# Attention, norm and MLP in one kernel: 1 KB input pieces for batch 0, and the loads of the second batch and of both weights in another order

## The chip, the cores and the metric

The kernel runs on one core of a Trainium2 chip. The metric is the device time of one execution in microseconds (us). A run counts as fast unless it lies more than 1.5% above the fastest run of the same kernel. In the profiles PE is TensorE (PEld its weight loads), DVE is VectorE, ACT is ScalarE, POOL is GpSimd and SP is SyncE; PSUM is the memory that the products are written to, and "busy" is the time in which an engine ran instructions. Verdicts are at 2%: a change that gains less is called "same".

## The reference, cut to what matters

Eight batches of eight heads of causal attention (576 positions, 64 wide) with a bias from running sums of `s`, then, on the joined heads, a norm scaled by `g_ln`, an up product with relu, a down product, and a residual.

```python
scores = scale * np.matmul(q, k.transpose(0, 1, 3, 2))
cum = np.cumsum(np.maximum(s, 0.0), axis=-1)
bias = -(cum[:, :, :, None] - cum[:, :, None, :])
scores = np.where(causal, -1e9, scores + np.minimum(bias, 0.0))
x = softmax(scores) @ v                              # (8, 8, 576, 64), then joined to (8, 576, 512)
xn = (x - mu) / np.sqrt(var + 1e-06) * g_ln
out = x + np.maximum(xn @ w_ch1, 0.0) @ w_ch2        # w_ch1 512 x 2048, w_ch2 2048 x 512
```

## The kernel before

The 64 heads run one after the other; "head 11" below is head 3 of batch 1. From head 11 on, MLP products of the batch before are laid between a head's own products. q and k are transposed by TensorE and copied out of PSUM by DVE or ACT. The bias rides in the product as four extra rows: the running sums, split into three bf16 terms, and ones, so 68 rows instead of 64.

```python
QUADS = (1, 2)        # batches whose q and k come in 1 KB pieces (4 positions per partition)

def t_pe(b, h, engs=("dve", "dve")):       # q, then k, of one head into qkT
    if b in QUADS:
        return t_quads(b, h, engs)         # two copies that put the order right (68x512),
                                           # and a third for the last 64 positions (68x2x64)
    for j, eng in ((h, engs[0]), (H + h, engs[1])):
        ...                                # five transposes, one straight copy (68x640)
```

Inputs are issued by SP, in one queue, but for three of the first ones, which ACT issues; casts to bf16, causal masks and the issues of the weights (which are cast in flight) are POOL's. What stands where in the program is set by hooks: `at(g, pos, f)` runs `f` in head g.

```python
for c, g in enumerate((6, 6, 7, 7)):                    # w1 in four parts
    at(g, "a", lambda c=c: load_w1(c))
for h, g in enumerate((0, 0, 1, 1, 7, 7, 8, 8)):        # q, k, v of batch 1, head h
    at(g, "e", lambda h=h: b1_in(h))                    # (h == 2 also loads g, 256 KB)
for i, g in enumerate((10, 10, 11, 11)):                # w2 in four parts
    at(g, "b", lambda i=i: load_w2(i))
at(12, "c", lambda: split(2 * H, BH, nc.vector))        # the sums of batches 2 to 7
for g in (12, 13, 14):                                  # batch 2
    at(g, "a", lambda g=g: b2_in(g))
```

The softmax here doesn't subtract the row's maximum and nothing guards it: scores larger than these inputs give would overflow.

Of the kernel before, what the change touches and what calls it, by code (L numbers as in the profile page):

```python
# [16 lines left out]
def kernel(  # L17
# [36 lines left out]
    QUADS = (1, 2)  # L54
# [43 lines left out]

    scr = xbufs[0]
# [6 lines left out]
    nc.sync.dma_start(out=s_sb, in_=s.rearrange("b h s -> (b h) s"))  # L106

# [53 lines left out]
    def t_quads(b, h, engs):  # L161
        pts = [ps_m.tile([P, 2 * 512], BF16, name="pt", tag="pm") for _ in range(2)]
        tails = pts[1][0:DK, NF * P : NF * P + 2 * P].rearrange("r (j n) -> r j n", j=2)
        for i in range(2):
# [11 lines left out]
            "dve", qkT[b][0:DK, :, NF * P : S].rearrange("r (j h) n -> r j h n", j=2)[:, :, h, :],  # L176
            tails[:, :, 0:TL],
        )

    def t_pe(b, h, engs=("dve", "dve")):  # L180
        if b in QUADS:
            return t_quads(b, h, engs)
        for j, eng in ((h, engs[0]), (H + h, engs[1])):
            pt = ps_m.tile([P, 2 * 512], BF16, name="pt", tag="pm")
            for p in range(NT):
                nc.tensor.transpose(pt[0:DK, p * P : (p + 1) * P], aug[:, p, j, 0:DK], ident)  # L186
            copy(eng, qkT[b][0:DK, j, :], pt[0:DK, 0:SP_])
# [10 lines left out]
    def score_mms(g):  # L198
# [6 lines left out]
        def mm(o, kb, lo, hi):  # L205
            lhsT = qkT[b][0:DK, H + h, kb * P : (kb + 1) * P]
            w = 0
            if g < NPM and lo == kb * P:
                w = min(P, hi - lo)
                nc.tensor.matmul(  # L210
                    o[:, 0:w], lhsT=lhsT, rhs=qkT[b][0:DK, h, lo : lo + w], start=True, stop=False
                )
                nc.tensor.matmul(
                    o[:, 0:w], lhsT=ident, rhs=negm[:, 0:w], start=False, stop=True
                )
            if lo + w < hi:
                nc.tensor.matmul(  # L217
                    o[:, w:], lhsT=lhsT, rhs=qkT[b][0:DK, h, lo + w : hi], start=True, stop=True
                )
# [6 lines left out]
        mm(pot[:, 448:512], 4, 512, 576)  # L226
# [65 lines left out]
    def store(c, a, yo):  # L292
        if c >= B:
            b0 = 4 * (c - B) + 2 * a
            late.append((out[b0, NF * P : S, :], yo[0:TL]))
            late.append((out[b0 + 1, NF * P : S, :], yo[TL:P]))
        else:
            late.append((out[c, a * P : (a + 1) * P, :], yo))

    def stores(eng, keep=0):  # L300
        while len(late) > keep:
            o, i = late.pop(0)
            eng.dma_start(out=o, in_=i)
# [186 lines left out]
    def spin(n):  # L490
        for _ in range(n):
            nc.tensor.matmul(idle[:, 0:P], lhsT=ident, rhs=ident, start=True, stop=True)

    spin(44)
# [7 lines left out]
    pc = ps_m.tile([P, 512], F32, name="pc", tag="pm")  # L502
    for p in range(NT):
        nc.tensor.transpose(pc[:, p * BH : (p + 1) * BH], cum[:, p * P : (p + 1) * P], ident_f)
# [3 lines left out]
    pc_v = pc[:, 0 : NT * BH].rearrange("p (t c) -> p t c", c=BH)  # L508
# [13 lines left out]
    split(0, H, nc.vector, pc_v[:, :, 0:H], aug[:, :, H:HD, D1:DK])  # L522
# [5 lines left out]
    spin(8)  # L528
    t_pe(0, 0, ("act", "dve"))
    nc.scalar.copy(out=c8, in_=pc_v)  # L530

    def cum_quads():

        pq = ps_m.tile([P, 512], F32, name="pq", tag="pm")[:, 0 : NF * 3 * H]
        pq = pq.rearrange("p (t c) -> p t c", t=NF)
        cum_q = cum[0 : 3 * H, 0 : NF * P].rearrange("c (p t) -> c t p", t=NF)
        for p in range(NF):
            nc.tensor.transpose(pq[:, p, :], cum_q[:, p, :], ident_f[0 : 3 * H, 0 : 3 * H])
        qs = slice(QUADS[0] * H, (QUADS[-1] + 1) * H)
        nc.vector.tensor_copy(out=c8[:, 0:NF, qs], in_=pq[:, :, qs])  # L540
# [26 lines left out]
    def t_next(g):  # L567
        t_pe((g + 2) // H, (g + 2) % H, ("dve", "act" if g >= H else "dve"))
# [191 lines left out]
```

## Time and profile before

| | before |
|---|---|
| time, median of 3 runs (range) | 379.52 us (378.34 to 379.99) |
| the profiled run: time, span | 380.23 us, 378.5 us |
| PE busy over the span | 94% |
| start of heads 6, 11, 14, 16 | 23.25, 42.99, 59.58, 80.43 us |

The times were taken outside the profile and the span inside it, so the span is 1.7 us shorter. The starts are the first score product of each head in the trace's order of time. The profiled run is at the slow end of the runs of its kernel. The lines of the profile itself stand in the prediction (those of the trace: start, length, instruction, wait in brackets).

Two stretches; the columns are stretch, length, busy PE, PEld, DVE, ACT, POOL, clock, DMA share and GB/s.

```profile
20.00:30.00 10.00, 8.73 (x157) 7.54 (x158) 7.98 (x22) 5.87 (x12) 3.62 (x9) 1.00 0.60 159
52.00:56.00 4.00, 2.55 (x15) 1.20 (x14) 3.90 (x6) 2.23 (x4) 4.00 (x7) 1.00 0.60 81
```

In these two stretches the DMA engines are 60% busy. The second hole has its reason in POOL's order of time (start, length, instruction, wait in brackets):

```profile
51.69 0.45 POOL L127 CAST v_bf<-ring 128x320 bf16<-128x320 f32 x1 [2.24 <-DMA ring<-in_v_dram]
52.08 1.57 POOL L151 DMA_DIRECT2D w_bf<-in_moe_w_ch_dram  x2
```

### The profile page before, as it was taken

Reading aid. Unit: us, or ns where it says so; the run is one execution under the profiler, and the core shown is the slowest. Engines: PE = TensorE matmul, PEld = TensorE weight load, DVE = VectorE, ACT = ScalarE, POOL = GpSimd, SP = SyncE. Lnnn points to the kernel's source line nnn. Section 1 sums busy time; section 2 is a strip of 40 time slices with the busy share of each in tenths; the row PEclk is TensorE's granted clock in tenths of the full one; section 3 lists DMA queues with packets and bytes.
Section 4 is the critical chain, followed back from the end, with each engine's and each line's share of the span. In section 5 each row is a group of like instructions: output and inputs, shape, how many; then the busy total and the mean of one; then the engine's idle time right before and its main releaser. Section 6 shows DMA issues by size and latency. Waiting matters only on the chain.

```text
span 378.5 us, 7931 instructions
## 1 busy us (share of the span) xinstructions
PE 354.7 (94%) x3017; PEld 204.5 (54%) x3017; DVE 201.9 (53%) x466; ACT 163.9 (43%) x295; POOL 167.6 (44%) x328
## 2 busy tenths in 40 slices
PE   6987878888999999999999999999999999899994
PEld 5966645455555455545555755555555555344471
DVE  6788575765454544594447435733555353933131
ACT  3755755154563457335632546444623554031020
POOL 3537964493634545575455544463444111500000
PEclk9998999999999999999999999999999999999998
DMA  9958989997999789999999999599804001420202
GB/s 164 207 150 190 221 143 187 245 248 176 176 227 227 137 198 211 229 198 205 174 210 239 174 246 224 119 195 207 156 29 113 29 2 55 113 55 0 86 28 55
DMA packets 175253, 59.12 MB, mean 156 GB/s; under 512 B 162224, under 2 KB 170416, under 8 KB 175216
## 3 DMA queue, kind: packets, MB, share of 16 engines
q1 hardware_dynamic: 165200, 46.43, 63.5%
q0 software_dynamic: 4224, 4.19, 7.0%
q10 hardware_dynamic: 5792, 8.00, 6.3%
q8 instruction: 23, 0.38, 0.4%
q14 instruction: 14, 0.11, 0.1%
HBM read 37.11 MB, written 9.44 MB: 123 GB/s over the span
## 4 chain that ended last, share of the span: by engine, by line
PE 75%; DMA 11%; DVE 6%; SPq 4%; issue 2%; POOL 1%; ACT 0%; DVEq 0%; POOLq 0%; ACTq 0%
PE ph L373 29%; PE py L384 28%; PE s L217 9%; PE pot L264 6%; DMA ring<-in_q_dram 4%; DMA ring<-in_v_dram 4%; DVE xn L323 2%; SPq L430 2%; DMA ring<-in_k_dram 1%; DVE stats L308 1%; DMA xnT<-xn 1%; SPq L422 1%; SPq L434 1%; DVE x L273 1%; PE pt L186 1%
## 5 line engine op out<-in xcount | busy, mean ns | idle before, releaser
L233 ACT ACTIVATE e<-s 128x1024 bf16<-128x1024 f32 (+1 forms) x128 | 99.0, 808 | 88.0 <-PE s L217 86.2
L384 PE MATMUL py<-w_bf,hT 128*128 128x512 bf16 x576 | 133.4, 379 | 0.0
L373 PE MATMUL ph<-xnT,w_bf 128*128 128x512 bf16 x512 | 120.7, 379 | 1.7 <-DMA xnT<-xn 1.7
L236 POOL TENSOR_SCALAR_AFFINE_SELECT e<-e 128x384 bf16<-128x384 bf16 x104 | 45.7, 464 | 111.2 <-ACT e L233 102.6
L358 DVE TENSOR_SCALAR hT<-ph 128x512 bf16<-128x512 f32 x72 | 49.6, 690 | 77.0 <-PE ph L373 76.4
L373 PEld LDWEIGHTS <-w_bf 128*128 128x128 bf16 x640 | 58.2, 98 | 50.3 <-issue 2.2
L384 PEld LDWEIGHTS <-hT 128*128 128x128 bf16 x576 | 53.1, 98 | 56.1 <-DVE hT L358 0.2
L356 ACT ACTIVATE hT<-ph 128x512 bf16<-128x512 f32 x72 | 43.0, 597 | 79.6 <-PE ph L373 77.3
L217 PE MATMUL s<-qkT 68*128 68x64 bf16 (+5 forms) x320 | 54.5, 287 | 0.0
L127 POOL CAST aug<-ring 128x512 bf16<-128x512 f32 (+2 forms) x85 | 44.4, 547 | 15.0 <-DMA ring<-in_k_dram 7.3
L390 DVE SCALAR_TENSOR_TENSOR yo<-py,rstd,x 128x512 f32<-128x512 f32 x32 | 24.0, 749 | 47.7 <-PE py L384 45.5
L217 PEld LDWEIGHTS <-qkT 68*128 68x128 bf16 x372 | 32.5, 98 | 24.7
L264 PEld LDWEIGHTS <-e 128*128 128x128 bf16 x960 | 37.9, 98 | 13.6 <-POOL e L236 1.1
L264 PE MATMUL pot<-v_bf,e 128*128 128x65 bf16 x960 | 40.1, 194 | 1.4 <-POOL e L236 1.0
L273 DVE TENSOR_TENSOR x<-pot,rinv 128x320 f32<-128x320 f32 x64 | 31.5, 492 | 2.9 <-DMA out_dram<-yo 0.5
L125 DVE COPY qkT<-pt 68x512 bf16<-68x512 bf16 (+2 forms) x49 | 21.9, 468 | 12.5 <-PE pt L166 4.4
L308 DVE BATCH_NORM_STATS2 stats<-x 128x6 f32<-128x256 f32 (+2 forms) x68 | 23.4, 398 | 0.3
L323 DVE SCALAR_TENSOR_TENSOR xn<-x,mv,gln_b 128x512 bf16<-128x512 f32 x32 | 23.2, 766 | 0.0
L127 POOL CAST v_bf<-ring 128x512 bf16<-128x512 f32 (+2 forms) x33 | 19.5, 613 | 2.2 <-DMA ring<-in_v_dram 2.2
L272 DVE RECIPROCAL rinv<-pot 128x5 f32<-128x5 f32 x64 | 12.0, 187 | 15.0 <-PE pot L264 14.9
L329 POOL TENSOR_TENSOR rstd<-rstd,nhalf 128x2 f32<-128x2 f32 x18 | 18.6, 1031 | 1.5
L166 PE MATMUL pt<-ident,aug 128*68 128x128 bf16 x128 | 11.8, 226 | 6.8 <-POOL aug L127 3.1
(78 smaller groups left out, 217.8 us busy)
## 6 DMA issues: line engine op xcount, KB each, us to landing
out_dram<-yo ACTq DMA_DIRECT2D x27, 256.0 KB, 3.3
ring<-in_q_dram SPq DMA_DIRECT2D x20, 256.0 KB, 4.9
ring<-in_k_dram SPq DMA_DIRECT2D x20, 256.0 KB, 4.8
ring<-in_v_dram SPq DMA_DIRECT2D x20, 256.0 KB, 4.3
w_bf<-in_moe_w_ch_dram POOLq DMA_DIRECT2D x8, 512.0 KB, 9.7
ring<-in_k_dram SPq DMA_DIRECT2D x30, 128.0 KB, 4.2
ring<-in_q_dram SPq DMA_DIRECT2D x22, 128.0 KB, 4.7
x<-in_v_dram SPq DMA_DIRECT2D x17, 128.0 KB, 4.0
```

What stands on the lines that cost most here:

```text
L127: nc.gpsimd.tensor_copy(out=o, in_=i)
L217: nc.tensor.matmul(o[:, w:], lhsT=lhsT, rhs=qkT[b][0:DK, h, lo + w : hi], start=True, stop=True)
L233: nc.scalar.activation(out=o, in_=i, func=ACT.Exp, scale=scale)
L236: nc.gpsimd.affine_select(out=d, in_=d, compare_op=ALU.is_ge, fill=0.0, base=0, pattern=[[0, d.shape[1]], [1, P]], channel_multiplier=-1,)
L264: nc.tensor.matmul(pot[:, t * D1 : (t + 1) * D1], lhsT=e[:, c : c + P], rhs=v_bfs[b % 2][:, kb, h, :], start=(kb == 0), stop=(kb == t),)
L273: nc.vector.tensor_tensor(out=xs[b][:, :, h * D : (h + 1) * D], in0=pv[:, :, 0:D], in1=rv.to_broadcast([P, NT, D]), op=ALU.mult,)
L308: nc.vector.bn_stats(out=sts[c, a][:, part, :], in_=x_of(c, a)[:, lo:hi])
L323: eng.scalar_tensor_tensor(out=xn[:, j, :], in0=x_of(c, a), scalar=mv[:, j, 0:1], in1=gln_b, op0=ALU.subtract, op1=ALU.mult,)
L356: nc.scalar.activation(out=o, in_=i, func=ACT.Relu)
L358: nc.vector.tensor_scalar_max(out=o, in0=i, scalar1=0.0)
L373: nc.tensor.matmul(ph[:, j * tok : (j + 1) * tok], lhsT=w1_bf[:, kd, fb * P : (fb + 1) * P], rhs=xnT[c][:, :, kd, :], start=(kd == 0), sto ...
L384: nc.tensor.matmul(st["py"], lhsT=st["h"][:, fb, a * P : (a + 1) * P], rhs=w2_bf[:, fb, :], start=(fb == 0), stop=(fb == FB - 1),)
```

## The change

Its intent: give the first batch larger pieces so that it arrives sooner, bring batch 1 in whole before the weights take their share of the DMA, and take 256 KB of broadcast g off the DMA.

```diff
-    QUADS = (1, 2)
+    QUADS = (0, 1, 2)
...
+    nc.gpsimd.dma_start(out=gln_r, in_=moe_g_ln.rearrange("(o f) -> o f", o=1))   # 2 KB
+    nc.gpsimd.memset(ones_r, 1.0)
... t_pe is gone, t_quads gets an engine for its third copy
-    spin(44)                       # warm-up products of 128 columns
+    spin(11)                       # of 512 columns
... the sums of batches 0 to 2 are transposed first (pq), all of them in head 1 (cum_all)
+    def spread_g():
+        pg = ps_m.tile([P, 512], F32, name="pg", tag="pm")
+        nc.tensor.matmul(pg, lhsT=ones_r, rhs=gln_r, start=True, stop=True)
+        nc.vector.tensor_copy(out=gln_b, in_=pg)
...
     def t_next(g):
-        t_pe((g + 2) // H, (g + 2) % H, ("dve", "act" if g >= H else "dve"))
+        t_quads((g + 2) // H, (g + 2) % H,
+            ("act" if g in(9,10) else "dve", "act" if g >= H else "dve", "dve"))
+    at(1, "c", cum_all)
+    at(3, "c", spread_g)
...
-    for c, g in enumerate((6, 6, 7, 7)):                  # w1
+    for c, g in enumerate((7, 7, 8, 8)):
-            nc.sync.dma_start(out=gln_b, in_=moe_g_ln.partition_broadcast(P))
-    for h, g in enumerate((0, 0, 1, 1, 7, 7, 8, 8)):      # batch 1
+    for h, g in enumerate((1, 1, 1, 1, 3, 3, 3, 3)):
-    for i, g in enumerate((10, 10, 11, 11)):              # w2
+    for i, g in enumerate((9, 9, 10, 10)):
... the last score product of a head (into pot) goes behind the next heads' transposes
... the two stores of one output tile are queued as a pair
```

So the change has more parts than its two main ones: g is spread by TensorE, the warm-up has another shape, the q copies of heads 11 and 12 go to ACT (`g in(9,10)`), and the last score product of each head moves.

One thing the diff does not say: SP's queue holds nothing but loads here, so the order of batch 0, 1 and 2 on it is the same in both kernels. What "batch 1 ahead of the weights" moves is the weights, on POOL, relative to POOL's casts.

More of the change, by code (lines that the diff above doesn't have):

```diff
@@ L97 @@
     xnT_tail = const.tile([P, 2, KD, P], BF16, name="xnT_tail")
+    gln_r, ones_r = xts[0][0:1, :], xts[2][0:1, Dm - P : Dm]
     scr = xbufs[0]
@@ L175, in t_quads @@
         copy(
-            "dve", qkT[b][0:DK, :, NF * P : S].rearrange("r (j h) n -> r j h n", j=2)[:, :, h, :],
+            engs[2],
+            qkT[b][0:DK, :, NF * P : S].rearrange("r (j h) n -> r j h n", j=2)[:, :, h, :],
             tails[:, :, 0:TL],
         )
-    def t_pe(b, h, engs=("dve", "dve")):
-        if b in QUADS:
-            return t_quads(b, h, engs)
-        for j, eng in ((h, engs[0]), (H + h, engs[1])):
-            pt = ps_m.tile([P, 2 * 512], BF16, name="pt", tag="pm")
-            for p in range(NT):
-                nc.tensor.transpose(pt[0:DK, p * P : (p + 1) * P], aug[:, p, j, 0:DK], ident)
-            copy(eng, qkT[b][0:DK, j, :], pt[0:DK, 0:SP_])
     def t_dma(b, p):
@@ L206, in mm @@
             lhsT = qkT[b][0:DK, H + h, kb * P : (kb + 1) * P]
-            w = 0
-            if g < NPM and lo == kb * P:
-                w = min(P, hi - lo)
-                nc.tensor.matmul(
-                    o[:, 0:w], lhsT=lhsT, rhs=qkT[b][0:DK, h, lo : lo + w], start=True, stop=False
-                )
-                nc.tensor.matmul(
-                    o[:, 0:w], lhsT=ident, rhs=negm[:, 0:w], start=False, stop=True
-                )
-            if lo + w < hi:
-                nc.tensor.matmul(
-                    o[:, w:], lhsT=lhsT, rhs=qkT[b][0:DK, h, lo + w : hi], start=True, stop=True
-                )
+            cuts = sorted({lo, hi, min(hi, lo + P) if g < NPM and lo == kb * P else hi})
+            for c0, c1 in zip(cuts[:-1], cuts[1:]):
+                d = o[:, c0 - lo : c1 - lo]
+                m = g < NPM and c0 == kb * P
+                nc.tensor.matmul(d, lhsT=lhsT, rhs=qkT[b][0:DK, h, c0:c1], start=True, stop=not m)
+                if m:
+                    nc.tensor.matmul(
+                        d, lhsT=ident,
+                        rhs=negm[:, 0 : c1 - c0],
+                        start=False, stop=True,
+                    )
         mm(s01[:, 0:512], 0, 0, 512)
@@ L225, in score_mms @@
         mm(s23[:, 320:512], 3, 384, 576)
-        mm(pot[:, 448:512], 4, 512, 576)
+        return lambda: mm(pot[:, 448:512], 4, 512, 576)
     def score_exp(g, part):
@@ L294, in store @@
             b0 = 4 * (c - B) + 2 * a
-            late.append((out[b0, NF * P : S, :], yo[0:TL]))
-            late.append((out[b0 + 1, NF * P : S, :], yo[TL:P]))
+            late.append(
+                [(out[b0, NF * P : S, :], yo[0:TL]), (out[b0 + 1, NF * P : S, :], yo[TL:P])]
+            )
         else:
-            late.append((out[c, a * P : (a + 1) * P, :], yo))
+            late.append([(out[c, a * P : (a + 1) * P, :], yo)])
     def stores(eng, keep=0):
         while len(late) > keep:
-            o, i = late.pop(0)
-            eng.dma_start(out=o, in_=i)
+            for o, i in late.pop(0):
+                eng.dma_start(out=o, in_=i)
     def stats(c, a, part, lo, hi):
@@ L491, in spin @@
         for _ in range(n):
-            nc.tensor.matmul(idle[:, 0:P], lhsT=ident, rhs=ident, start=True, stop=True)
-    spin(44)
+            nc.tensor.matmul(
+                idle, lhsT=ident,
+                rhs=ident.rearrange("p (o n) -> p o n", o=1).to_broadcast([P, 4, P]),
+                start=True, stop=True,
+            )
+    spin(11)
     nc.vector.tensor_scalar(
@@ L501 @@
     )
-    pc = ps_m.tile([P, 512], F32, name="pc", tag="pm")
+    NQ = len(QUADS) * H
+    pq = ps_m.tile([P, 512], F32, name="pq", tag="pm")[:, 0 : NT * NQ]
+    pq = pq.rearrange("p (t c) -> p t c", t=NT)
+    cum_q = cum[0:NQ, 0 : NF * P].rearrange("c (p t) -> c t p", t=NF)
     for p in range(NT):
-        nc.tensor.transpose(pc[:, p * BH : (p + 1) * BH], cum[:, p * P : (p + 1) * P], ident_f)
+        nc.tensor.transpose(
+            pq[:, p, :], cum_q[:, p, :] if p < NF else cum[0:NQ, NF * P : SP_],
+            ident_f[0:NQ, 0:NQ],
+        )
     c8, r8 = (
@@ L507 @@
     )
-    pc_v = pc[:, 0 : NT * BH].rearrange("p (t c) -> p t c", c=BH)
     def split(lo, hi, eng, a=None, o=None):
@@ L521 @@
     cast_head("k", 0, 0, "pool")
-    split(0, H, nc.vector, pc_v[:, :, 0:H], aug[:, :, H:HD, D1:DK])
+    split(0, H, nc.vector, pq[:, :, 0:H], aug[:, :, H:HD, D1:DK])
     nc.scalar.activation(
@@ L527, with cum_all @@
     cast_head("k", 0, 1, "pool")
-    spin(8)
-    t_pe(0, 0, ("act", "dve"))
-    nc.scalar.copy(out=c8, in_=pc_v)
-    def cum_quads():
-        pq = ps_m.tile([P, 512], F32, name="pq", tag="pm")[:, 0 : NF * 3 * H]
-        pq = pq.rearrange("p (t c) -> p t c", t=NF)
-        cum_q = cum[0 : 3 * H, 0 : NF * P].rearrange("c (p t) -> c t p", t=NF)
-        for p in range(NF):
-            nc.tensor.transpose(pq[:, p, :], cum_q[:, p, :], ident_f[0 : 3 * H, 0 : 3 * H])
-        qs = slice(QUADS[0] * H, (QUADS[-1] + 1) * H)
-        nc.vector.tensor_copy(out=c8[:, 0:NF, qs], in_=pq[:, :, qs])
+    spin(2)
+    t_quads(0, 0, ("act", "dve", "act"))
+    nc.scalar.copy(out=c8[:, :, 0:NQ], in_=pq)
+    def cum_all():
+        pc = ps_m.tile([P, 512], F32, name="pc", tag="pm")
+        pc_v = pc[:, 0 : NT * BH].rearrange("p (t c) -> p t c", c=BH)
+        for p in range(NT):
+            nc.tensor.transpose(pc_v[:, p, :], cum[:, p * P : (p + 1) * P], ident_f)
+        nc.vector.tensor_copy(out=c8[:, :, NQ:BH], in_=pc_v[:, :, NQ:BH])
+    def spread_g():
+        pg = ps_m.tile([P, 512], F32, name="pg", tag="pm")
+        nc.tensor.matmul(pg, lhsT=ones_r, rhs=gln_r, start=True, stop=True)
+        nc.vector.tensor_copy(out=gln_b, in_=pg)
     cast_head("q", 0, 2, "dve")
@@ L567, in t_next @@
     def t_next(g):
-        t_pe((g + 2) // H, (g + 2) % H, ("dve", "act" if g >= H else "dve"))
-    at(0, "a2", lambda: t_pe(0, 1))
-    at(0, "a2", cum_quads)
+        t_quads(
+            (g + 2) // H, (g + 2) % H,
+            ("act" if g in(9,10) else "dve", "act" if g >= H else "dve", "dve"),
+        )
+    at(0, "a2", lambda: t_quads(0, 1, ("dve", "dve", "dve")))
+    at(1, "c", cum_all)
+    at(3, "c", spread_g)
     at(2, "c", lambda: split(H, 2 * H, nc.vector))
@@ L589, in b1_in @@
     def b1_in(h):
-        if h == 2:
-            nc.sync.dma_start(out=gln_b, in_=moe_g_ln.partition_broadcast(P))
         heads_in(1, (h,))
@@ L605, in t_act @@
     def t_act(b, h):
-        t_pe(b, h, ("dve", "act"))
+        t_quads(b, h, ("dve", "act", "dve"))
     def c_head(b, h):
@@ L630 @@
         at(6 + p, "e", lambda p=p: nc.gpsimd.memset(aug[:, p, :, DK:P], 0.0))
+    B2 = 12
     def b2_in(g):
-        if g == 12:
+        if g == B2:
             for what in "qkv":
                 tails_in(what, 2, nc.sync)
-        heads_in(2, range(3 * (g - 12), min(H, 3 * (g - 12) + 3)))
-    for g in (12, 13, 14):
+        heads_in(2, range(3 * (g - B2), min(H, 3 * (g - B2) + 3)))
+    for g in (B2, B2 + 1, B2 + 2):
         at(g, "a", lambda g=g: b2_in(g))
@@ L711 @@
         if g < NG:
-            score_mms(g)
+            score_tail = score_mms(g)
             run(g, "a2")
+            score_tail()
             score_exp(g, 0)
```

## The prediction

> **What bounds the kernel now.** I read the time strip first, then busy time by stretch, then the chain of waits up to 80 us, then the timelines of PE, DVE and POOL there.
>
> ```profile
> PE   6987878888999999999999999999999999899994
> PEclk9998999999999999999999999999999999999998
> DMA  9958989997999789999999999599804001420202
> ```
>
> One digit is 9.5 us. From slice 11 on TensorE is full; the gaps, and the dip of its clock, lie in the first 95 us.
>
> ```profile
> 10.00:20.00 10.00, 9.60 (x166) 8.59 (x164) 7.70 (x22) 7.16 (x13) 6.38 (x15) 1.00 1.06 208
> 30.00:40.00 10.00, 7.05 (x93) 5.76 (x91) 8.47 (x27) 5.70 (x10) 8.27 (x13) 0.83 0.96 189
> 55.00:60.00 5.00, 2.54 (x32) 1.80 (x33) 3.87 (x10) 0.80 (x2) 4.29 (x8) 1.00 1.12 174
> 70.00:80.00 10.00, 6.97 (x52) 3.74 (x50) 7.73 (x19) 2.92 (x5) 7.22 (x15) 1.00 0.85 228
> 140.00:200.00 60.00, 60.00 (x497) 32.20 (x495) 32.74 (x74) 29.15 (x54) 33.09 (x63) 1.00 1.12 208
> ```
>
> Columns: stretch, length, busy PE, PEld, DVE, ACT, POOL, clock, DMA share, GB/s. PE is full from 140 to 200 us; it loses 3.0, 2.5 and 3.0 us in the middle three. DVE is busy 7.7 of 10 us already at 10 to 20; I return to that.
>
> ```profile
> 2.59 5.58 DMA ring<-in_q_dram
> 26.93 5.11 DMA ring<-in_k_dram
> 37.46 14.17 DMA ring<-in_v_dram
> 61.32 9.03 DMA ring<-in_q_dram
> ```
>
> The chain's four long pieces before 80 us are loads: batch 0; batch 1's first half; its second half, in flight together with the first weight; batch 2, together with the second. On the engines:
>
> ```profile
> 32.18 0.46 POOL L127 CAST aug<-ring 128x320 bf16<-128x320 f32 x1 [1.32 <-DMA ring<-in_k_dram]
> 32.69 0.41 PE L166 MATMUL pt<-ident,aug 128*68 128x128 bf16 x4 [1.30 <-POOL aug L127]
> 56.50 0.38 PE L166 MATMUL pt<-ident,aug 128*68 128x128 bf16 x4 [1.95 <-DVE hT L358]
> 70.38 0.49 DVE L125 CAST aug<-ring 128x320 bf16<-128x320 f32 x1 [0.72 <-DMA ring<-in_q_dram]
> ```
>
> The first two are one wait: load, POOL cast, PE transposes. The third is not a load: DVE is held 3.5 us (52.3 to 55.8) by the four-step split of the sums. The fourth is DVE waiting for batch 2.
>
> Where each head's first score product starts gives the loss by head. Head 0 starts at 9.36 us, 6 at 23.25, 8 at 29.29, 10 at 37.37, 11 at 42.99, 13 at 51.98, 14 at 59.58, 15 at 64.17, 16 at 80.43. Undisturbed heads last 2.0 us without MLP units (head 1: 1.99) and 4.3 to 4.6 with three or four. So heads 6, 8, 9 and 10 lose about 1.8, 2.2, 1.8 and 2.7, head 13 about 3.3, head 15 almost 4.
>
> **What the Trainium skill says.** "DMA: Bandwidth & Descriptors", the section on why small descriptors are slow, says that each operation carries fixed overhead. The trace agrees: 256 B packets have a median of 18 ns (14 B/ns), 1 KB ones 46 ns (22 B/ns). The same page, on queues and rings, says that an engine round-robins between its queues by packet. Agrees: between 62 and 64 us 306 weight packets (96 ns median) and 307 input packets of 256 B went out, one for one. "VectorE: DVE Perf Modes", on PSUM operands, caps what is read from PSUM at a lower tier; the trace alone shows what an order-changing read costs on top:
>
> ```profile
> L125 DVE COPY qkT<-pt 68x512 bf16<-68x512 bf16 x18 | 12.2, 681 | 4.6 <-PE pt L166 4.4
> L125 DVE COPY qkT<-pt 68x640 bf16<-68x640 bf16 x15 | 6.7, 481 | 3.8 <-PE pt L186 3.7
> L125 DVE COPY qkT<-pt 68x128 bf16<-68x128 bf16 x16 | 3.5, 217 | 4.1 <-ACT qkT L123 4.1
> ```
>
> "TensorE: Matmul & The Clock Gate", part 1, lets activity of about 3.4 us release the clock. The 44 warm-up products of 128 columns took 4.03 us, as 3.4 us at half clock and the rest at full would; eleven of 512 columns have the same 5632 columns, so I expect no change there.
>
> **The change part by part.** (1) q and k of batch 0 in 1 KB pieces. A 128 KB load is 32 packets of 18 ns on each of 16 engines (0.58 us) before and 8 of 46 ns (0.37) after: 16 x 0.21 = 3.4 us of DMA time. But issuing takes about 0.55 us per load, so the 25 issues last to about 15.4 us, against 18.3 before. At the start, ACT's copy of q (8.63) sat behind a cast waiting for q of head 1 (landed 8.18); that wait goes, the copy of k (8.27, set by the sums) remains. Head 0 starts near 8.9: gain 0.45.
>
> (2) The price. Heads 0 to 5 change from two straight copies (0.89 us together; 0.80 from one start to the next instruction) to two reordering copies and a tail copy (1.33 to 1.42 at heads 6 and 7 of before). With reciprocal and scaling (0.65), DVE needs 1.98 us per head where it needed 1.45. Moved or added on DVE: copying all sums about 0.35 (head 1), g out of PSUM about 0.65 (head 3). Kept: split 1.16, shift 0.4, stats 1.3. PE gets 0.85 for spreading g (an fp32 64-column product took 0.1, this has 512); the DMA of 256 KB for g goes.
>
> I ran DVE forward from 9.3 us with these durations, letting PE wait where its scores need DVE's copies or its output banks DVE's scaling: head 1 at 11.4 us, 2 at 13.9, 3 at 15.9, 4 at 18.8, 5 at 20.9, 6 at 23.4, 7 at 25.8, 8 at 29.1, 9 at 31.6, 10 at 34.1, 11 at 39.0. DVE is never idle between 10 and 38 us. So the early data is not worth its 10 us of waits: head 6 starts where it did (23.25), head 11 gains 4.0 against 42.99. Giving head 11's and 12's q copies to ACT saves DVE 1.2 us at the norm and is in this sum.
>
> (3) Batch 1 whole ahead of the weights. Its 30 issues run from 15.4 to about 31 us, half a us each; head h of it lands near 18 + 1.5h, before PE asks. w1 is issued when POOL has cast its fourth head, about 26, so the last three heads still share with w1 packet for packet: 144 packets at about 0.12 us end near 44, against 52.6 before. POOL then casts v of head 15 about 45, before head 12's masks are ready, and the 0.96 us that PE waited for a mask at head 13 goes. The DVE split at head 12 stays, and its 2 us. Heads 11, 12 and 13: 4.7 + 4.3 + 6.4, so head 14 starts at 54.4 against 59.58: gain 5.2.
>
> (4) Batch 2 starts loading when k of batch 1 is cast, about 45 instead of 55.5, and its first heads land near 58 to 60 instead of 69 to 70.4. Head 15 starts at 59.0 and DVE asks at about 62.5: the two waits there (1.14 and 0.72 us) go, and about 2.0 us of PE's idle with them. Sum at head 16: 7.2. Everything after is full, same work, same order of units; the last chunk's transpose wait (1.7) and the tail of 58 us do not change. The tail of scores moved behind the transposes is in the sums above.
>
> 379.5 - 7.2 = 372.3. PE's clock should not halve near 35 us (3.4 us at 0.5 before), which my head lengths assume already; head 17's 1.34 us stall may also go. I say 371.5.
>
> **Rivals.** First: loads were the bound, so nearly all the loss in heads 6 to 15 comes back: 1.8 + 2.2 + 1.8 + 2.7 + 1.3 + 2 + 0.5, about 12 us, 367. The chain speaks for it; the DVE sum against, since 8.5 of 10 us are already busy at 30 to 40. Second: DVE cancels it. If the triple costs 1.6 us (the first one at head 6 took 1.63), eight heads lose another 2 us, and if g or the sums run long, 1 more: 375. The gap-free DVE sum speaks for it. Third: the weights become the wait. w2's last pieces land near 58 here; the first is needed at the end of head 15, about 63. That holds in my order, but if POOL, whose queue puts head 7's copy and the norm's power ahead of w2, is 5 us later, PE stops at the first down product: 373 to 374. Fourth: the gain is given back later, batch 3's loads being on time only by luck. Against: no cast waits for a load after 80 us; and both move together.
>
> **Range and chances.** The DVE pitch (0.1 us over ten heads), POOL's lateness and head 15 give about 2.5 us each way; the first rival sets the low end. 367.5 to 376. The 2% line is 371.9, nearly on my estimate: faster 0.53, same 0.44, slower 0.03; nothing here costs 7 us without a new wait.
>
> **What would show it.** DVE over 9 of 10 us busy between 10 and 38, the trio near 1.35, head 6 within 1 us of 23.4 and head 11 of 39; batch 1 landed by 45, batch 2's q of head 1 by 60, no DVE wait for it; a DVE-held transpose at head 13 still there; lengths equal from head 18. Wrong if head 11 starts before 37 or after 41, if PE waits for a weight, or if heads 18 on lengthen.

## The result, and the profile after

The ratio is the mean time of one kernel's fast runs over that of the other's in the same rounds, so it is not quite the ratio of the medians.

| | before | changed | ratio (95%) |
|---|---|---|---|
| first measurement, 4 runs each | 378.93 (377.94 to 379.99) | 373.80 (372.52 to 375.42) | 0.9866 (0.9817 to 0.9916) |
| second, 11 and 5 runs | 379.09 (377.28 to 380.39) | 373.79 (373.00 to 374.15) | 0.9861 (0.9833 to 0.9889) |

The change gains 1.35 to 1.4%, "same" at 2%. It lies inside the predicted range, 2.3 us above the predicted time. The profiled run took 373.61 us with a span of 371.8.

The time strip of the changed kernel (one digit is 9.3 us):

```profile
PE   7997989898999999999999999999999999899994
PEclk9999999999999999999999999999999999999998
DMA  8979999895999499999996999499404001520202
```

Of PE's ten digits ahead of slice 11 six are one higher and none is lower, and the dip in the clock is absent. The same stretches as in the prediction, and the two holes of above:

```profile
10.00:20.00 10.00, 9.74 (x162) 8.31 (x159) 8.59 (x24) 6.83 (x14) 6.17 (x15) 1.00 0.91 225
20.00:30.00 10.00, 8.81 (x162) 7.67 (x162) 9.84 (x29) 6.60 (x12) 6.73 (x15) 1.00 0.75 181
30.00:40.00 10.00, 8.20 (x151) 7.23 (x147) 9.20 (x31) 8.70 (x19) 9.82 (x17) 1.00 1.12 193
52.00:56.00 4.00, 3.17 (x37) 2.09 (x37) 3.20 (x10) 1.42 (x3) 2.15 (x5) 1.00 1.24 206
55.00:60.00 5.00, 5.00 (x42) 2.65 (x41) 3.40 (x9) 2.96 (x6) 1.99 (x5) 1.00 1.22 213
70.00:80.00 10.00, 9.13 (x87) 5.99 (x86) 5.98 (x13) 5.73 (x11) 9.66 (x23) 1.00 1.00 239
```

PE gains about 1.2 us at 30 to 40, 2.5 at 55 to 60 and 2.2 at 70 to 80; DVE is now the fullest engine at 20 to 30; the hole in the loads at 52 to 56 is closed (81 to 206 GB/s). From 140 to 200 us PE is full, 60.00 of 60 us, as before. Head by head:

| head starts at (us) | 0 | 6 | 8 | 10 | 11 | 14 | 16 | 18 |
|---|---|---|---|---|---|---|---|---|
| before | 9.36 | 23.25 | 29.29 | 37.37 | 42.99 | 59.58 | 80.43 | 94.21 |
| predicted | 8.9 | 23.4 | 29.1 | 34.1 | 39.0 | 54.4 | 73.2 | |
| changed | 9.81 | 24.56 | 29.99 | 35.02 | 39.35 | 54.96 | 73.95 | 87.39 |
| changed, second profile | 9.36 | 24.04 | | | 38.84 | 55.09 | 74.08 | 87.53 |

The gain by stage, from the first and third row: 0.45 lost before head 0, 0.9 lost from head 0 to 6, 4.95 won from 6 to 11, 1.0 from 11 to 14, 1.9 from 14 to 16, 0.3 from 16 to 18, and 0.1 lost after it: 6.7, the difference of the spans.

The chain of waits of the changed kernel has one long load left before 75 us, where it had four:

```profile
59.84 3.48 DMA x<-in_v_dram
```

Of the four waits in the prediction, the second (PE for POOL's cast) and the fourth (DVE for a load) have no successor. POOL still waits for q and k of batch 1, up to 1.47 us at 26.32, but PE no longer waits for those casts. New or left in PE's order of time are these:

```profile
29.47 0.20 PE L207 MATMUL pot<-qkT 68*128 68x64 bf16 x1 [0.87 <-DVE x L267]
52.18 0.38 PE L170 MATMUL pt<-ident,aug 128*68 128x128 bf16 x4 [1.12 <-DVE hT L353]
```

The first is head 7: the head's last score product wants a bank that DVE's scaling of two heads ago has yet to read. Heads 8, 9 and 10 have 0.44, 0.27 and 0.88 us of it; 2.5 us in all, at the heads where DVE also computes the first norm. The second is what was 1.95 us: DVE's split at head 12. Head 13 has a second wait, and its reason is in POOL's order of time:

```profile
46.83 0.46 POOL L131 CAST v_bf<-ring 128x320 bf16<-128x320 f32 x1 [1.88 <-DMA ring<-in_v_dram]
47.23 1.56 POOL L155 DMA_DIRECT2D w_bf<-in_moe_w_ch_dram  x2
...
52.53 0.47 POOL L131 CAST v_bf<-ring 128x320 bf16<-128x320 f32 x1 [1.78 <-DMA ring<-in_v_dram]
52.95 1.73 POOL L230 TENSOR_SCALAR_AFFINE_SELECT e<-e 128x384 bf16<-128x384 bf16 x4
```

The last v of batch 1, issued at 37.20, landed only at 52.48; before it was 52.62. POOL waits for it, the causal masks stand behind its cast, and PE waits 0.65 us for a mask. In the second profile of the changed kernel PE came to head 13 half a us sooner, v landed at 52.61, and the wait for the mask was 1.64; head 14 started at 55.09. In both profiles head 14 starts 2.48 us after that v has landed. For batch 2 DVE waits no more:

```profile
63.33 0.87 DVE L129 CAST aug<-ring 128x320 bf16<-128x320 f32 x2
```

Both casts of q run back to back, with no bracket; the second q had landed at 62.82. The costs of the copies out of PSUM (busy, mean ns of one, idle before them) are as predicted:

```profile
L129 DVE COPY qkT<-pt 68x512 bf16<-68x512 bf16 x31 | 20.4, 681 | 5.7 <-PE pt L170 5.0 <-PE pt L173 0.6
L129 DVE COPY qkT<-pt 68x128 bf16<-68x128 bf16 x23 | 4.9, 214 | 2.8 <-ACT qkT L127 2.8
```

Three things were open. Is it DVE that sets the pace up to head 11, as the prediction says, or was the gain limited by loads? Which half of the change, the pieces or the order, brought the gain? And what holds heads 13 and 14: the split on DVE, or v?

### The profile page after: what moved, and what is told of

It reads as the page before. It is cut to its first block, busy times and chain, and to the rows that moved or that the text cites. A ratio compares the mean times of both kernels' runs of the same rounds, so it can differ in the third digit from the quotient of the medians.

```text
span 371.8 us, 7869 instructions
## 1 busy us (share of the span) xinstructions
PE 353.7 (95%) x2981; PEld 200.8 (54%) x2981; DVE 202.6 (54%) x472; ACT 164.5 (44%) x298; POOL 169.0 (45%) x331
## 4 chain that ended last, share of the span: by engine, by line
PE 74%; DVE 6%; DMA 2%; SPq 2%; issue 1%; ACT 1%; POOL 0%; ACTq 0%; DVEq 0%
PE ph L368 30%; PE py L379 28%; PE s L207 8%; PE pot L258 6%; DVE xn L318 2%; DMA xnT<-xn 1%; DVE stats L303 1%; DMA x<-in_v_dram 1%; SPq L425 1%; PE pt L170 1%; DVE yo L385 1%; DVE x L267 1%; DVE qkT L129 0%; ACT e L227 0%; PE pot L207 0%
## 5 line engine op out<-in xcount | busy, mean ns | idle before, releaser
L207 PE MATMUL s<-qkT 68*128 68x192 bf16 (+5 forms) x368 | 55.4, 277 | 0.8 <-DVE qkT L129 0.8
L207 PEld LDWEIGHTS <-qkT 68*128 68x128 bf16 x432 | 36.8, 97 | 30.7 <-DVE x L267 2.9
L258 PEld LDWEIGHTS <-e 128*128 128x128 bf16 x960 | 37.1, 98 | 12.4 <-POOL e L230 0.8
L129 DVE COPY qkT<-pt 68x512 bf16<-68x512 bf16 (+1 forms) x54 | 24.2, 482 | 8.5 <-PE pt L170 5.0
L303 DVE BATCH_NORM_STATS2 stats<-x 128x6 f32<-128x256 f32 (+2 forms) x68 | 23.4, 398 | 0.3
L131 POOL CAST v_bf<-ring 128x512 bf16<-128x512 f32 (+2 forms) x33 | 18.3, 578 | 3.7 <-DMA ring<-in_v_dram 3.7
L266 DVE RECIPROCAL rinv<-pot 128x5 f32<-128x5 f32 x64 | 12.0, 187 | 14.6 <-PE pot L258 14.5
L170 PE MATMUL pt<-ident,aug 128*68 128x128 bf16 x192 | 16.4, 219 | 3.0 <-DVE qkT L129 1.4
```

Of the source, the lines that this page charges most:

```text
L131: nc.gpsimd.tensor_copy(out=o, in_=i)
L207: nc.tensor.matmul(d, lhsT=lhsT, rhs=qkT[b][0:DK, h, c0:c1], start=True, stop=not m)
L258: nc.tensor.matmul(pot[:, t * D1 : (t + 1) * D1], lhsT=e[:, c : c + P], rhs=v_bfs[b % 2][:, kb, h, :], start=(kb == 0), stop=(kb == t),)
```

## The experiments

The record marks every kernel below as correct, even the one with straight copies, which is wrong: q and k are drawn at 0.1, so their scaled products are about 0.01 (an estimate from the reference), and the check does not notice their order. It therefore vouches for the order of q and k in none of these runs. Those with one run have the state "unknown" and are read by their trace, not by their time. A caution for all of them: the clock of TensorE went to half in some profiles and not in others, for times near 3.4, 6.8 or 10.2 us. A profile with such a dip cannot show a small difference behind it, and I say where there was one. The dips go with PE's gaps: cut into stretches of 3.41 us on the grid of the clock's changes, the 14 traces have 1386 stretches at full clock in which PE was busy for more than 68%, and none was followed by half clock; of the 59 with 68% or less, 14 were. The dip of the kernel before, at 35.2 us, followed a stretch of 64%. Why the other 45 had no dip after them is open.

**The warm-up as before.** The changed kernel with 44 (and later 8) products of 128 columns.

```diff
-    spin(11)        # of 512 columns
+    spin(44)        # of 128 columns
```

> The changed kernel with the old warm-up (44 and 8 products of 128 columns instead of 11 and 2 of 512). In the profile of the change the clock was released at 7.1 us instead of 4.5, the warm-up took 4.87 us instead of 4.03 and head 0 started at 9.81 instead of the 8.9 that I predicted. If the shape of the warm-up does this: release near 4.5 us again, head 0 near 8.9, total about 0.9 us less than the change's 373.8. Rival, the release falls by chance[...]: no difference in time beyond 0.5 us, and a release time that varies from profile to profile with either shape.

Measured: 372.78 us (4 runs, 372.34 to 374.45), ratio 0.9863 (0.9810 to 0.9917), the change's own ratio. Head 0 started at 9.37 and head 11 at 39.24. The clock was released at 4.17 us, against 7.14 in the changed kernel's first profile and 5.22 in its second. But over the profiles the old shape gave 4.50, 4.17, 5.05, 6.50 and 7.33, the new one 4.22 to 7.56. The release time varies with either shape, and the shape moves nothing that could be resolved.

**The order alone.** The kernel before, with only the new places for batch 1 and both weights.

```diff
-    w1 (6, 6, 7, 7)    batch 1 (0, 0, 1, 1, 7, 7, 8, 8)    w2 (10, 10, 11, 11)
+    w1 (7, 7, 8, 8)    batch 1 (1, 1, 1, 1, 3, 3, 3, 3)    w2 (9, 9, 10, 10)
```

> The kernel before with the places of the loads alone (batch 1 at heads 1 and 3, w1 at heads 7 and 8, w2 at 9 and 10); batch 0 stays in 256 B pieces with straight copies. On the load queue of SP the order of batch 1's loads is the same in both kernels, so only the weights' place behind POOL's casts moves. My theory (the pieces of 1 KB bring batch 1's first half forward, the weights' place does little): heads 6 and 8 wait as before, head 11 starts within 1.5 us of 43, total 377 to 379. Rival (the order of the loads is what pays): head 11 near 39 to 40, total 374.

Measured: 376.22 us (4 runs), ratio 0.9948 (0.9905 to 0.9991), between my expectation and its rival. Head 10 started at 34.17 instead of 37.37, although nothing about batch 0 had changed. As I read the order on POOL, the two pairs of w1's issues, about 1.6 us each, now stand ahead of the casts of batch 1's heads 4 and 5 instead of 3 and 4; I did not test that by itself. Then head 10 lasted 6.40 and head 11 5.52 us, partly in a clock dip from 39.2 to 42.6 (a second one ran from 56.3 to 59.7), and head 11 started at 40.57. Ahead of the first dip, at 37.15, PE waits 1.91 us for DVE's scaling where the changed kernel waits 0.88: this kernel has neither the moved score product nor ACT's copies of q.

**The pieces alone.** The changed kernel with the old places of batch 1 and the weights (and the transposes of all sums in head 0, as before). It keeps all the rest of the change, not the pieces alone: g by TensorE, the new warm-up, the moved score product and ACT's copies of q.

> The changed kernel with the old places of the loads and weights; pieces of 1 KB, reordering copies and g by TensorE kept. My theory: heads 6 to 10 as in the change (head 10 within 1 us of 35), total 373.5 to 375. Rival (order pays): w1 shares with batch 1 from earlier on, head 11 at 41 or later, total 376 or more.

Measured: 376.45 us (4 runs), ratio 0.9949 (0.9904 to 0.9993), worse than the range expected. Its profile holds a clock of 0.51 from 10 to 20 us:

```profile
10.00:20.00 10.00, 10.00 (x96) 8.85 (x94) 5.33 (x12) 4.05 (x8) 5.99 (x14) 0.51 0.91 221
```

PE is busy all of the ten and gets through 96 products, where the changed kernel got through 162. Head 6 started 4.2 us later than in the changed kernel, yet the span is only 2.9 longer. So the trace of this run can't be set against the others head by head; its timed runs can, and they say that the order and all the rest are worth 0.5% each and the whole 1.35 to 1.4%. The product of the two ratios is 0.9897; with half-widths of 0.0043 and 0.0044, that is not shown to differ from 0.9861. Whether the halves help each other stays open; that neither half is the whole gain is clear. What the pieces bring without the smaller parts beside them was not measured.

**The third copies on ACT.** Meant to take 0.2 us per head off DVE at heads 1 to 9.

```diff
-            ("act" if g in(9,10) else "dve", "act" if g >= H else "dve", "dve"),
+            (..., "dve" if g >= H else "act"),
```

> The changed kernel with the small tail copy (0.2 us) of each head from 1 to 9 on ACT instead of DVE. If DVE sets the pace between 10 and 38 us: eight or nine times 0.15 to 0.2 us less on DVE, PE's waits for DVE's scaling at heads 7 to 10 (0.87, 0.44, 0.27, 0.88 us) shrink, head 11 starts near 38 instead of 39.35, total 372.3 to 373. Rival, PE or ACT sets the pace (ACT goes from 1.74 to 2.0 us per head): no gain or a loss of up to 1 us.

Measured: 389.50 us, ratio 1.0278 (1.0217 to 1.0340), slower. In order of time:

```profile
38.83 0.26 ACT L127 COPY qkT<-pt 68x128 bf16<-68x128 bf16 x1 [2.11 <-DVE qkT L129]
...
38.99 1.50 ACT L227 ACTIVATE e<-s 128x1024 bf16<-128x1024 f32 x2
40.06 0.22 PE L207 MATMUL s<-qkT 68*128 68x128 bf16 x1 [1.74 <-ACT e L227]
```

ACT's copy waits 2.11 us for DVE's copy of k, ACT's exponential stands behind it, and PE's next scores wait 1.74 us for that exponential, since there is one score buffer. The profile has the clock at half from 14.5 to 17.9, 24.8 to 31.6 and 45.3 to 48.7 us, and its four runs a mean clock of 0.962 to 0.981, so part of the loss is the clock's; the lines above lie where it was full. This says nothing on DVE's load; I had built a new chain. An engine with room in its busy time is not free if its next instruction is the one that PE waits for.

**g by DMA again.** The changed kernel without the spreading product; g comes by its 256 KB load.

> The changed kernel with g spread by the old load of 256 KB in the middle of batch 1, not by TensorE. Head 3 lasts 3.13 us in the change, 1.1 more than its neighbours: 0.85 for the fp32 product on PE, and 0.68 of DVE for its copy. If DVE sets the pace to 38 us: heads 1 to 10 together 0.7 to 1.1 us shorter, total 0.7 to 1 us less. Rival, the load costs more than it saves (0.9 us of load time ahead of batch 1's second half, half a us of issue): head 3 about 2.1, but head 8 or later waits for a cast and head 11 does not start earlier than 39.35.

Measured: one run, 373.04 us, beside 378.49 for the kernel before. Head 3 lasted 1.98 us instead of 3.13, and head 11 started 0.66 earlier. Head 14 started at 53.79, which is 2.49 us after the last v of batch 1 had landed, at 51.30; in the kernel with the old warm-up these were 54.36 and 51.89, 2.47 us apart. In time, 5.45 us off the kernel before against 5.1 to 5.3 for the whole change, one run shows nothing of the price of spreading g.

**The split in two.** To take it out of head 13's way: 8 columns at head 12, the other 40 at head 14.

```diff
-    at(12, "c", lambda: split(2 * H, BH, nc.vector))
+    at(12, "c", lambda: split(2 * H, 3 * H, nc.vector))
+    at(14, "c", lambda: split(3 * H, BH, nc.vector))
```

> The changed kernel with the split of the sums of batches 3 to 7 moved from head 12 to head 14; only batch 2's stays at head 12. If DVE's 2.8 us of split is what holds head 13 (6.48 us instead of 4.3; PE waits 1.12 for DVE): head 13 about 4.9 to 5.3, its wait for the mask (0.65) left or larger; the rest of the split moves into head 15, where DVE had room: total 0.5 to 1.2 us less. Rival, the mask behind the late load of v holds head 13 anyway, or head 15 gives it back: total unchanged within 0.5.

Measured: one run, 378.88 us, with a clock dip from 55.7 to 59.2 and one near 330, so its time tells nothing. What it does tell is DVE's and POOL's order of time at head 12:

```profile
49.02 0.90 DVE L519 CAST cumh<-xt 128x40 bf16<-128x40 f32 x1
49.96 0.36 DVE L520 TENSOR_TENSOR xt<-xt,cumh 128x40 f32<-128x40 f32 x1
50.35 0.98 DVE L521 CAST cumh<-xt 128x40 bf16<-128x40 f32 x1
```

```profile
48.80 1.57 POOL L155 DMA_DIRECT2D w_bf<-in_moe_w_ch_dram  x2
50.34 0.94 POOL L640 MEMSET aug<- 128x960 bf16 x1
```

The same split of 8 columns, at head 2 of the changed kernel:

```profile
18.34 0.43 DVE L519 CAST cumh<-xt 128x40 bf16<-128x40 f32 x1
18.80 0.20 DVE L520 TENSOR_TENSOR xt<-xt,cumh 128x40 f32<-128x40 f32 x1
19.04 0.20 DVE L521 CAST cumh<-xt 128x40 bf16<-128x40 f32 x1
```

Steps of the same size took about twice as long or, in the third, five times, where POOL issues w2 and clears a buffer at the same time. A smaller split was thus no cheaper one here. The kept traces show the other side: with no issue and no clearing beside it, the whole split of 48 columns took 1.9 us (weights later, pieces alone), against 2.8 in the changed kernel and 3.6 before. So what the split cost went with what POOL did beside it. PE's wait for a mask was there too (1.91 us), v having landed at 53.95.

**The third copies twice.** If DVE sets the pace, nine copies more, at 0.214 us 1.9 us in all, must show at head 11.

```diff
-        copy(engs[2], ...)
+        for _ in range(2 if 0 < b * H + h < 10 else 1):
+            copy(engs[2], ...)
```

> The changed kernel with the tail copy of heads 1 to 9 done twice on DVE: nine times about 0.15 to 0.2 us more DVE and nothing else. If DVE sets the pace: head 11 starts 1.2 to 1.8 us later than 39.35 after correction for head 0's start, 40.6 to 41.1. If PE or the loads set it: less than 0.5 us later.

Measured: one run, 374.00 us, no clock dip. Head 11 started at 41.06, 1.7 us later than in the changed kernel. Head 14 started at 55.21, 0.25 later. The wait at head 13 is where it went:

```profile
53.34 0.38 PE L170 MATMUL pt<-ident,aug 128*68 128x128 bf16 x4 [0.57 <-DVE hT L354]
```

It is now the only wait of that head. In the changed kernel the end of head 13 followed v; here v landed at 50.01, PE did not wait for it, and head 13 lasted 5.02 us instead of 6.48. (v itself was issued at 35.77 instead of 37.20, and w2's first part at 41.48 instead of 39.77; which of the two brought v sooner is not separated.) So the 1.7 us that DVE had cost were nearly made up at head 13. DVE sets the pace up to head 11, and little of that pace reaches the end. Over 10 to 38 us DVE was as busy as before the doubling (changed kernel first, then this one):

```profile
10.00:38.00 28.00, 24.95 (x440) 21.64 (x438) 26.21 (x77) 20.13 (x40) 20.72 (x42) 1.00 0.91 199
```

```profile
10.00:38.00 28.00, 24.27 (x415) 20.64 (x412) 26.21 (x81) 18.70 (x36) 19.06 (x40) 1.00 0.92 203
```

26.21 of 28 us both times: DVE is at its limit, and with more per head it does less of the rest (PE 415 products instead of 440).

**The pieces with straight copies.** Batch 0 arrives in 1 KB pieces, is copied straight and so stays in the wrong order. This gives the early data without DVE's price. It is the order-alone kernel with one line:

```diff
-        if b in QUADS and what != "v":
+        if b in (0, 1, 2) and what != "v":
```

> The kernel before with the new places of loads and weights, and batch 0's q and k in pieces of 1 KB but copied straight, so that its result is wrong on purpose. It has the early data without the reordering copies. My theory (the reordering copies on DVE eat the early data): heads 1 to 5 at 2.0 to 2.3 us each, head 6 near 22.5 to 23, head 11 at 36.5 to 37.5, two us or more ahead of the change's 39.35. Rival (DVE's copies are hidden; loads or the norm at heads 8 to 10 set head 11): head 11 within 0.7 us of 39.35.

Measured: one run, 377.88 us, with the clock halved from 9.9 to 16.7 and from 40.6 to 47.5, so the time is of no use. Heads 2 to 9, which all lie between the dips (17.2 to 36.8), lasted 19.56 us together, against 19.98 in the changed kernel and 19.3 in the one without the spreading of g. No time was won back, while the doubling above shows that adding to DVE's work costs. But this is not a clean test of the price. The kernel also keeps the old place of the last score product: in its heads 2, 4 and 5, of 2.13 to 2.24 us, DVE stood idle for 0.61 us ahead of a copy of q, so DVE was not the limit there, and undisturbed heads of the kernel before (3 and 5) took 2.13 too. Its heads 6 to 9, for which the copies are nearly alike in both kernels, took 10.92 us against 10.48 without the spreading of g. What straight copies would bring with the new place of that product is open.

**The weights later.** The changed kernel with w1 and w2 two heads later.

```diff
-    w1 (7, 7, 8, 8)      w2 (9, 9, 10, 10)
+    w1 (9, 9, 10, 10)    w2 (11, 11, 12, 12)
```

> The changed kernel with w1 at heads 9 and 10 and w2 at 11 and 12: batch 1 now lands truly before the weights. If packets are shared one for one, v of batch 1's last head lands at 37 to 40 instead of 52.5. But w1 is issued at about 38 to 39 and is wanted at about 41: PE waits 2 to 4 us for it at heads 11 to 12 (the third rival of the prediction made real), total 374.5 to 377. If the late v is not due to sharing: it lands within 3 us of 52.5.

Measured: one run, 378.48 us, with a clock dip from 41.8 to 48.6. The last v of batch 1 landed at 37.57 instead of 52.48. Head 11 started at 39.35, just as in the changed kernel, and then lasted 11.14 us, a good part of it in the dip:

```profile
45.24 1.03 PE L368 MATMUL ph<-xnT,w_bf 128*128 128x512 bf16 x2 [4.76 <-DMA w_bf<-in_moe_w_ch_dram]
```

That is the third rival of the prediction, made real by two heads. It shows both sides: with no weight in flight v is issued 4 us sooner (33.18 instead of 37.20) and lands 15 us sooner, and the weight is then what PE waits for.

**The changed kernel again.**

> The changed kernel itself once more, for a time beside the next two and for more samples of the clock. 373.8 as before within 1 us; single runs spread by 2 to 3 us, the slower ones at a lower mean clock, if the spread comes from clock windows lost in the first 60 us.

Measured: the second row of the result's table. The mean clocks of its five runs were 0.998, 0.992, 0.997, 0.998 and 0.997, and the fastest run (373.00) is the one with the lowest. A lower mean clock did not go with a longer run here, nor in the kernel before, where 0.988 goes with 377.28 us and 0.995 with 380.05. The changed kernel's mean clock is a little higher (0.995 over nine runs, against 0.991 over 19), but nothing here puts the gain down to that.

**w2 in its old place.** Everything else changed.

```diff
-    for i, g in enumerate((9, 9, 10, 10)):
+    for i, g in enumerate((10, 10, 11, 11)):
```

> The changed kernel with w2 alone back at heads 10 and 11. In the change v of batch 1's last head lands at 52.5 us, while w1 and w2 are in flight from 29 to 59, and POOL's mask for head 12 waits behind its cast; where w2 was issued after 47 us (pieces alone) that v landed at 46.7 and head 13 lasted 4.63 instead of 6.48. If the sharing with w2 is what holds head 13: v lands near 46 to 47, head 13 lasts 4.6 to 5.4, head 15 up to 0.5 us longer because batch 2 then shares with w2; total 0.7 to 1.8 us less than the change in the same rounds. Rival (DVE's split of the sums holds head 13): head 13 above 5.8, total equal.

Measured: 374.89 us (6 runs, 374.53 to 376.12), ratio 0.9901 (0.9871 to 0.9931), 1.1 us worse than the change in the same rounds, where I had expected 0.7 to 1.8 better. Its profile has a clock dip from 10.2 to 13.6, which makes head 11 start at 40.06. The last v of batch 1 landed at 46.31 instead of 52.48. Head 13 shrank from 7.12 us in the second profile of the changed kernel to 5.09, and only DVE's wait is left in it. Then head 15 gave it back, 16.11 us instead of 14.39, with DVE in wait of batch 2 (1.30 us, and 0.41 for the next q at 64.94):

```profile
52.41 0.38 PE L170 MATMUL pt<-ident,aug 128*68 128x128 bf16 x4 [0.64 <-DVE hT L353]
```

```profile
64.04 0.49 DVE L129 CAST aug<-ring 128x320 bf16<-128x320 f32 x1 [1.30 <-DMA x<-in_v_dram]
```

The same bytes in another order: what was won at head 13 was lost at head 15.

**The three together.** The old warm-up, g by DMA and w2 in its old place, in the hope of a version that beats the change.

> The changed kernel with w2 at heads 10 and 11, g by the old load and the old warm-up. Sum of what single runs gave: about 1.2 (w2), 0.5 (g), 0.5 to 1 (warm-up): 371 to 372, two to three us less than the change in the same rounds. If the gains are the same wait seen three times, 373.

Measured: 376.82 us (6 runs, 374.48 to 377.80), ratio 0.9938 (0.9906 to 0.9970): 3 us worse than the change in the same rounds, where I had expected about 2 us better. Its profile has a clock dip from 10.7 to 14.2, head 13 of 6.08 and head 15 of 16.84 us, so head 15's loss is there again. Its loads are all later than with w2 in its old place alone: w1's first issue at 30.34 instead of 27.63, the last v landed at 48.86 instead of 46.31, w2's first issue at 47.86 instead of 45.69, and DVE waits 1.89 and 0.56 us for batch 2. The 256 KB of g, back in SP's queue, may be why; that was not tested, so the 2 us by which it is worse stay unexplained. No version beat the changed kernel.

## Why the prediction was right or wrong

**What was right.** The time lay in the range, 373.8 against 371.5; but it fell on the "same" side of the 2% line, to which I had given 0.44, and not on the "faster" side with 0.53. The forward sum for DVE held: predicted 34.1 and 39.0 for heads 10 and 11, measured 35.02 and 39.35, with 1.41 us for the three copies of a head (1.33 to 1.42 predicted) and DVE busy 26.21 of 28 us, though not without a gap, and only 8.59 of the first ten. The doubled copies confirm DVE's pace up to there. The first rival (all of the loads' waits come back, 367) fell for the reason given: PE waits 2.5 us for DVE at heads 7 to 10. The second (DVE cancels the gain) fell because the three copies cost what they cost before and not 1.6 us. The third did not happen in the changed kernel, and two heads' delay of the weights made it happen. From head 18 on nothing changed, as predicted (0.1 us). Of the signs that I had named, three failed: head 6 within 1 us of 23.4 (24.56, and 24.04 in the second profile), batch 1 landed by 45 (52.48), and batch 2's q of head 1 by 60 (62.82).

**Step 1, head 0 at 8.9, was wrong.** It started at 9.81, and at 9.36 or 9.37 in two profiles whose clock was released earlier. The wait for a late q is gone, but I had left two terms out. The copy of k that the first scores wait for is now an order-changing one, 0.69 us where it was 0.49. And the sums that it follows left TensorE later: DVE could start on them at 7.15 us, or 6.61 in the two other profiles, where it was 6.26. The transposes of the sums, now of 24 columns, took 0.69 to 0.78 us where those of 64 took 0.49. In the first profile, moreover, the warm-up itself, at half clock, ran to 6.40 us, past the end of DVE's running sum at 5.74; in the second it ended at 5.88. The gain of 0.45 did not come. The offset of about 0.9 in the first profile runs through to head 10, and 0.35 of it is left at head 11. Spreading g took PE 1.13 us, not 0.85.

**Step 3 gave the right sum for a wrong reason.** Heads 11 to 13 were to last 15.4 us and lasted 15.6. But I let the last v of batch 1 land near 44, took away the wait for a mask and kept 2 us for the split. It landed at 52.48, the wait for the mask stayed (0.65 and 1.64), and the wait for the split was 1.12. The mis-sized term is the sharing with the weights. I counted 144 packets shared with w1 to about 44 and left w2 out, whose first issue, at 39.77, came while that v, issued at 37.20, was in flight. w1 itself was issued at 28.76, not 26, and the last issue of batch 1 was that of this v, at 37.20 and not near 31. Two runs show the sharing: with w2 a head later v landed at 46.31, and with both weights later at 37.57. (In both v was also issued sooner, at 36.26 and 33.18.) And four profiles show what v sets: in both of the changed kernel, with the old warm-up and with g by DMA, head 14 starts 2.47 to 2.49 us after v has landed, though head 11 started anywhere from 38.69 to 39.35.

**Step 4 was right in kind and early in time.** The first loads of batch 2 were issued at 50.8 instead of 45 and the second q landed at 62.8 instead of 58 to 60, still before DVE asked. The two waits of DVE went, and heads 14 and 15 together gained 1.9 us (2.0 predicted). The margin was thin: with w2 a head later DVE waited 1.30 and 0.41 us.

**Where the 2.3 us are.** At head 16 the trace gained 6.5 us, where I had 7.2: in the sum, 0.9 lost at head 0, 0.55 won from there to head 11, and 0.2 lost in each of the next two stages. Since v sets the start of head 14, the 0.7 cannot be put down to head 0. I added 0.8 for the clock near 35 us and for a stall at head 17; after head 16 only 0.2 came. That makes 6.7 instead of 8.0. The rest is the base: the profile of before that I read the losses from was of a run of 380.23 us, with a clock dip, and I subtracted them from a median of 379.52. 380.23 less 6.6 (the difference of the profiled runs) is 373.6. So one profile's losses were 6.6 us, where the medians differ by 5.1 to 5.3. How much of that difference is the clock dip alone I could not settle.

**The explanation that stands.** Before, most of PE's gaps at heads 6 to 15 came from loads that waited behind one another and from POOL, which stood before a late v with the next weight's issue behind it. The change took this out at heads 6 to 10 and at 14 to 16. What is left has two limits in a row: DVE to head 11 (more work on it delays that head; what less would bring is open), and at head 13 the last v of batch 1 together with DVE's split. The second can hide what is won or lost ahead of it. That the loads as a whole are the limit of what is left to win is argued from three orders (v late in the changed kernel, batch 2 late with w2 in its old place, w1 late with both later), each of which only moved the wait; no run with fewer bytes was made to show it.

## What to carry to other kernels

When several loads are shared out among later users, write down for each order which one lands last and who asks for it first; moving one ahead moves another back, and the sum over all users is what counts. A price that is paid ahead of a later wait can vanish in it, and so can a gain: test it by doubling the price and see whether the difference is still there some stages on. Subtract losses read from one profile only from the time of that run, and check first whether its clock dipped.

## What the Trainium skill lacked or had wrong

- "DMA: Bandwidth & Descriptors", "Queues, rings and completion order": the turn-taking by packet is stated and agrees with the trace; what it does to one small load is not. A 128 KB load with casting loads of both weights in flight, some issued before it and some after, landed 15.3 us after the start of its issue (37.20 to 52.48), and the same load with no weight in flight 4.4 us after it (33.18 to 37.57).
- "VectorE: DVE Perf Modes", "Why PSUM operands drop a tier": it has no time for a read from PSUM that changes the order. A straight copy of 68x640 took 481 ns, an order-changing one of 68x512 took 681 ns: 0.75 against 1.33 ns per column.
- "SBUF — State Buffer", "Who interferes with whom": it calls the port pair that DVE and GpSimd share an exclusive lock. The trace agrees in kind, in that a DVE step of 128x40 took 0.90 us beside POOL's issue of weights and 0.98 beside a memset, and 0.43 and 0.20 at head 2; the page gives no time for small steps beside an issue of weights. Beside issues alone the first step of the split took 0.90 us (the split in two) and 1.08 (before, 240 columns), but also 0.39 (the changed kernel's second profile, and w2 in its old place), which is what it took beside none: an issue can hold such a step, but need not, and what decides is open.
- "TensorE: Matmul & The Clock Gate", part 1: it calls the window free-running and variable from run to run, which agrees (release at 4.2 to 7.6 us over 14 profiles), and puts the warm-up's penalty under 1% of a span. That holds for the start; a return to half clock for 10.24 us soon after it went with a head 6 that was 4.2 us late in one run, 1.1% of its span, part of which was absorbed later. How idle TensorE must be for such a dip the page does not give as a share of busy time: here all 14 dips followed a stretch of 3.41 us with PE busy for 68% or less, and so did 45 stretches without one.
